# Six VectorE operations at other places of a hand-written order, and one PSUM tile in another bank

## The chip, the cores and the metric

The kernel runs on one core of a Trainium2 chip. The metric is the device time of one execution in microseconds. The engines are TensorE (PE, with its weight loads PEld), VectorE (DVE), ScalarE (ACT), GpSimd (POOL) and SyncE (SP). SP issues most DMAs and all transposing DMAs; POOL issues the DMAs that add to their destination.

## The reference, cut to what matters

The input is a sequence of 2048 positions with 640 channels. Two branches are computed from it and mixed by a sigmoid gate per position.

```python
def _A_ref(q, k, v, shift_k, ssm_k, ssm_D):      # long convolution
    k_shift = sum over 4 taps of shifted k times shift_k
    kv = k_shift * v
    y = irfft2(rfft2(kv padded) * rfft2(ssm_k padded))[:S]
    return q * (y + kv * ssm_D)

def _B_ref(x, w1, w2, w3, w4):                   # token-shift mixer and MLP
    h = gelu(layernorm(x) @ w1)
    x1 = x + concat(four quarters of h, shifted by 1, -1, 2, -2 positions) @ w2
    return x1 + gelu(layernorm(x1) @ w3) @ w4

g = sigmoid((x * gate_w).sum(-1))
out = g * a + (1 - g) * b                        # a, b: the two branches, x = A_q
```

## The kernel before

**The work.** Branch B runs over 16 tiles of 128 positions (names with t) or over 4 chunks of 512 positions (sc). `ln1` normalizes, `mm1` multiplies by w1, `mm2` by w2 and adds the residual (one VectorE operation per tile, a SCALAR_TENSOR_TENSOR at line 967 that reads PSUM), `ln2` normalizes again, `mm3` and `mm4` are the MLP, `base` stores a first part of the output. Branch A runs over 5 chunks of 128 channels (c). Its convolution is a folded discrete Fourier transform: `h_load` loads the filter, `h_fold` forms even and odd folds of it on VectorE and transposes them by a DMA, `h_even` and `h_chunk` finish its transform; `kv` does the same for the data (taps, product with v, fold, transposing DMA), `kv2` folds the transposed data once more (two operations, a sum and a difference), `x_fwd` transforms it on TensorE, `combine` prepares blocks. `unit(c)` multiplies the transforms block by block on VectorE: products go into two buffers TT[0] and TT[1] and are added to two accumulators, by VectorE (`tt`) or, where a bit of `ON` says so, by an accumulating DMA that POOL issues. `final` transforms back on TensorE, copies on ScalarE, folds on VectorE and stores.

**The order.** All operations are recorded one by one in the order of the source; an operation's number is its place in that record. Which operation depends on which is found from the memory they touch. `SEQUENCE` then lists all 1176 numbers in a hand-kept order. Each engine executes its own operations in the order in which they stand there, strictly one after the other; where an operation depends on one of another engine (or on an earlier one of its own, except on TensorE), `emit` puts a semaphore wait in front of it. A wait therefore holds everything behind it on that engine, and also, on SP, all DMAs behind it. `PLACES` gives each PSUM tile its first bank out of 8. A tile placed on a bank waits until the tile that was there before has been read:

```python
            if t is not None and t.place is None:
                t.place = places[t.idx]
                for b in range(t.place, t.place + t.n):
                    if tenant[b] is not None:
                        for u in tenant[b].users:
                            if ops[u].eng != "pe":
                                o.preds.setdefault(u, False)
                    tenant[b] = t
```

**The numbers that the text uses.**

| number | engine | what it is |
|---|---|---|
| 340 | DVE | `h_fold(1)`: main part of the second chunk's odd fold (128x1016) |
| 339, 341, 342 | DVE | small parts of the same fold; 343, a transposing DMA on SP, needs all of them and 340 |
| 290 to 293 | DVE | `h_even(0)` |
| 305, 306 | DVE | last two operations of `kv(0)`; 307 on SP transposes their result |
| 500, 504, 526, 508, 512, 530, 534 | DVE | `mm2`'s residual additions of tiles 0, 1, 4, 2, 3, 5, 6 |
| 230, 216 | PE | products whose PSUM tiles stand on the bank that 530 reads |
| 246, 256 | SP | transposes of the last chunk of `ln1`, behind 343 in SP's order |
| 390 | SP | load of the third chunk's filter, behind 256; 391 on DVE is the first to use it |
| 374, 375 | DVE | `kv2(1)`: the sum (374) and the difference (375) of the second chunk's even fold |
| 376 | PE | `x_fwd(1)`: first matmul that needs 374; 837 is the next `mm4` product |
| 637, 640 | POOL | accumulating DMAs of `unit(0)`, reading TT[0] |
| 639, 641 | DVE | `unit(0)`: product into TT[1] and its addition |
| 642, 643 | DVE | `unit(0)`: products into TT[0] and TT[1] |
| 644, 645 | DVE | additions of 642's and 643's products to the two accumulators |
| 646, 647, 648 | DVE, DVE, ACT | close the first half of `unit(0)`; 648 needs 647 |
| 649 to 654 | DVE | second half of `unit(0)`: 649, 650 first products; 651, 652 into TT[0], TT[1]; 653, 654 additions |
| 904, 905 | PE, ACT | `mm3(2)`: product into PSUM tile 149 and the gelu that reads it |
| 1021, 716 | PE | first matmuls into tiles 180 and 116, which follow on the banks concerned |

The product lines of the helper `tt` all appear at line 646, those of `act` at 656, the matmuls at 678, transposing DMAs at 234 and other DMAs at 237.

Of the kernel before, what the change touches and what calls it, by code (L numbers as in the profile page):

```python
# [433 lines left out]
def bass_gated_mix__ssm_conv_h3__mixer_s_mlp__prompt_kernel(  # L434
# [34 lines left out]
    def ps(n, cls):  # L469
# [4 lines left out]
                49, 14, 50, 131, 54, 15, 51, 36, 57, 55, 16, 66, 56, 17, 282, 65, 58, 18, 68, 336, 19, 69, 193, 20,  # L474
                67, 59, 71, 194, 41, 136, 21, 72, 42, 22, 70, 62, 60, 37, 133, 23, 61, 43, 35, 73, 135, 74, 295, 75,
                39, 63, 132, 83, 137, 64, 134, 81, 33, 76, 138, 78, 84, 139, 40, 91, 149, 82, 77, 87, 146, 97, 147,
                103, 150, 98, 79, 92, 88, 102, 80, 151, 95, 140, 107, 283, 148, 96, 105, 101, 108, 111, 152, 143,
                106, 119, 153, 44, 104, 286, 85, 120, 144, 112, 141, 123, 86, 145, 117, 154, 38, 99, 157, 155, 142,
                34, 113, 195, 158, 118, 196, 156, 166, 338, 114, 159, 168, 197, 198, 208, 109, 287, 337, 160, 100,
                288, 199, 169, 188, 167, 125, 284, 126, 110, 127, 128, 209, 180, 285, 289, 122, 93, 200, 206, 121,  # L480
                189, 201, 297, 190, 202, 191, 164, 94, 129, 207, 124, 182, 210, 298, 178, 181, 236, 165, 171, 192,
                89, 183, 172, 174, 161, 211, 299, 235, 179, 212, 162, 90, 175, 502, 203, 301, 503, 185, 186, 204,
                115, 170, 498, 205, 340, 213, 163, 499, 116, 300, 173, 214, 176, 291, 215, 524, 504, 525, 342, 500,
                505, 296, 302, 501, 506, 507, 177, 237, 184, 187, 510, 29, 526, 239, 30, 511, 508, 247, 349, 528,
                303, 240, 224, 249, 512, 220, 238, 304, 248, 532, 241, 225, 251, 306, 529, 221, 305, 533, 250, 242,
                290, 307, 243, 314, 513, 252, 317, 341, 530, 294, 318, 253, 293, 315, 292, 230, 319, 216, 339, 534,
                343, 316, 231, 245, 311, 312, 228, 232, 514, 217, 244, 233, 222, 255, 509, 246, 352, 234, 313, 218,
                515, 254, 516, 351, 223, 256, 308, 353, 219, 309, 331, 310, 332, 390, 320, 6, 328, 333, 321, 350,
                329, 322, 344, 323, 330, 271, 325, 226, 326, 272, 227, 273, 327, 274, 229, 265, 345, 324, 517, 355,
                261, 403, 519, 354, 259, 391, 393, 276, 266, 356, 522, 263, 275, 270, 518, 268, 277, 357, 257, 260,  # L490
                520, 521, 558, 278, 334, 279, 264, 559, 269, 358, 258, 554, 523, 348, 555, 267, 360, 262, 536, 359,
                406, 537, 560, 361, 371, 556, 372, 368, 346, 373, 369, 347, 395, 606, 576, 396, 281, 335, 370, 607,
                577, 538, 817, 365, 366, 392, 550, 367, 394, 551, 829, 608, 397, 562, 531, 552, 563, 527, 621, 635,
                535, 622, 539, 564, 602, 405, 540, 603, 632, 385, 386, 623, 823, 362, 387, 363, 541, 407, 542, 382,
                444, 383, 364, 604, 617, 409, 618, 633, 578, 816, 619, 824, 637, 384, 588, 543, 634, 579, 600, 408,
                445, 636, 592, 638, 548, 582, 399, 589, 640, 590, 398, 601, 547, 410, 584, 544, 549, 448, 596, 591,
                375, 585, 411, 594, 593, 597, 866, 598, 639, 595, 402, 422, 400, 641, 379, 583, 423, 380, 424, 586,
                446, 404, 401, 381, 642, 580, 643, 599, 587, 425, 644, 581, 426, 645, 416, 835, 651, 417, 419, 545,
                420, 646, 819, 818, 427, 449, 647, 546, 418, 374, 652, 820, 836, 648, 421, 457, 650, 376, 377, 872,
                837, 649, 378, 878, 458, 388, 561, 838, 654, 565, 653, 884, 447, 825, 412, 557, 553, 655, 839, 656,  # L500
                826, 821, 389, 657, 450, 566, 831, 661, 451, 460, 567, 414, 568, 413, 858, 827, 659, 415, 459, 832,
                663, 860, 830, 859, 658, 864, 867, 861, 665, 841, 462, 844, 879, 660, 667, 854, 865, 461, 845, 852,
                833, 569, 662, 463, 842, 453, 848, 664, 855, 856, 853, 464, 849, 666, 843, 862, 429, 857, 571, 465,
                850, 863, 669, 846, 851, 428, 574, 671, 452, 433, 847, 834, 434, 436, 466, 435, 439, 440, 455, 437,
                441, 430, 468, 431, 880, 467, 456, 668, 469, 570, 670, 881, 438, 454, 673, 572, 432, 672, 470, 625,
                443, 479, 882, 480, 674, 678, 473, 474, 914, 471, 676, 874, 481, 684, 873, 675, 472, 885, 475, 482,
                490, 491, 483, 493, 492, 677, 494, 886, 680, 495, 697, 679, 605, 442, 573, 887, 682, 609, 681, 575,
                487, 740, 888, 875, 683, 741, 484, 876, 485, 488, 738, 868, 489, 739, 486, 742, 869, 700, 689, 743,
                900, 610, 686, 699, 745, 894, 496, 908, 747, 624, 687, 611, 701, 870, 476, 906, 895, 685, 497, 901,
                890, 909, 744, 926, 620, 477, 927, 688, 892, 703, 690, 746, 691, 912, 626, 749, 627, 910, 891, 748,  # L510
                698, 478, 751, 612, 902, 907, 750, 920, 280, 752, 898, 911, 753, 903, 921, 896, 913, 757, 754, 758,
                904, 893, 755, 1008, 897, 915, 702, 988, 756, 989, 759, 999, 692, 760, 905, 1000, 628, 704, 840,
                899, 1021, 1001, 1022, 694, 990, 705, 716, 932, 717, 613, 1010, 629, 706, 933, 986, 1011, 630, 693,
                928, 980, 707, 718, 708, 766, 709, 696, 929, 1012, 762, 719, 761, 1023, 922, 1019, 767, 763, 614,
                1030, 764, 631, 930, 923, 962, 765, 768, 987, 720, 924, 769, 934, 615, 771, 616, 733, 695, 734, 723,
                773, 730, 735, 731, 889, 722, 935, 883, 732, 1013, 991, 931, 1002, 737, 916, 936, 1014, 721, 1003,
                770, 974, 917, 772, 918, 710, 711, 1024, 774, 712, 724, 919, 713, 1052, 714, 775, 725, 937, 1063,
                944, 715, 776, 822, 981, 727, 777, 1161, 728, 726, 1015, 950, 779, 1009, 778, 948, 784, 780, 992,
                945, 782, 960, 968, 956, 781, 961, 786, 729, 940, 1025, 1074, 783, 1016, 1086, 1064, 736, 938, 1098,
                949, 1041, 785, 957, 993, 946, 941, 1017, 963, 951, 792, 997, 1018, 939, 952, 1110, 994, 877, 1146,  # L520
                788, 947, 1004, 969, 871, 787, 942, 953, 975, 793, 1087, 1134, 789, 958, 1122, 790, 954, 959, 943,
                791, 1032, 794, 955, 828, 1020, 1033, 795, 1005, 982, 1034, 797, 998, 983, 995, 799, 1026, 964,
                1035, 1027, 801, 984, 1036, 1006, 803, 1031, 1028, 985, 965, 796, 1037, 798, 970, 966, 1038, 967,
                1099, 1039, 1053, 925, 800, 971, 1162, 1040, 1111, 802, 804, 976, 972, 805, 1147, 810, 996, 806,
                809, 973, 977, 808, 1112, 807, 978, 1100, 1101, 1042, 812, 979, 1113, 1102, 1043, 811, 1029, 1114,
                1044, 1103, 1075, 813, 1065, 1104, 1045, 814, 1066, 1135, 815, 1046, 1007, 1105, 1088, 1067, 1115,
                1047, 1089, 1116, 1106, 1068, 1048, 1076, 1107, 1049, 1077, 1069, 1090, 1108, 1136, 1050, 1078,
                1109, 1070, 1117, 1091, 1137, 1071, 1079, 1051, 1092, 1054, 1118, 1080, 1072, 1138, 1093, 1081,
                1119, 1055, 1094, 1139, 1073, 1082, 1120, 1163, 1140, 1056, 1121, 1083, 1141, 1164, 1095, 1142,
                1084, 1124, 1165, 1057, 1085, 1125, 1143, 1148, 1058, 1126, 1166, 1059, 1144, 1149, 1060, 1127,  # L530
                1145, 1096, 1150, 1128, 1097, 1061, 1129, 1130, 1151, 1170, 1123, 1062, 1155, 1167, 1156, 1168,
# [619 lines left out]
```

## Time and profile before

| | |
|---|---|
| median of 3 runs | 224.52 us (224.51 to 224.65) |
| profiled execution, its own time | 223.96 us |
| its span, first to last instruction | 222.1 us |
| busy: PE, DVE, ACT, POOL | 208.7, 211.7, 193.3, 54.2 us |
| mean granted TensorE clock | 0.995 |

The page of the profile gives shares of busy time, the chain of waits that ended last and the costliest groups. The timeline lists instructions in order of time, neighbours of one form merged, with the idle time before them and what ended it in square brackets; its first two columns are start and duration in us from the span's start. A stretch row gives, for a window of time, its length, the busy time and count of each engine, the granted clock, the share of the DMA engines and GB/s. A matmul's end is modelled in the records, so a full TensorE can still have small waits in it.

### The profile page before, as it was taken

The page shows a single profiled execution, that of the slowest core. Times are in us where ns is not written, and L with a number is a line of the kernel's source. Part 1 is how long each engine was busy: PE and PEld are TensorE (multiplying, and loading weights), DVE is VectorE, ACT ScalarE, POOL GpSimd, SP SyncE. Part 2 cuts the span into 40 slices and gives each one's busy share as a digit, 9 for nine tenths or more (in the row PEclk, how much of TensorE's full clock was granted, in tenths as well). Part 3 has the DMA queues.
Part 4 walks back from the last instruction along what each step waited for, and adds up shares of the span by engine and source line. Part 5 has one row for each costly group of instructions (what it writes and reads, how often), then busy time and mean ns, then how long its engine had stood idle before and what let it go on. Part 6 is the DMA issues. An engine that isn't in the chain of part 4 may idle for free.

```text
span 222.1 us, 3844 instructions
## 1 busy us (share of the span) xinstructions
PE 208.7 (94%) x1403; PEld 125.5 (57%) x1410; DVE 211.7 (95%) x417; ACT 193.3 (87%) x324; POOL 54.2 (24%) x57
## 2 busy tenths in 40 slices
PE   5899989989999999899999999999999999999970
PEld 2589755445665445565446575445667444677740
DVE  6999999989999986999999999999999999999993
ACT  2489999999899999799999999999977898566981
POOL 0512303200003100005130002164016427276431
PEclk9999999999999999999999999999999999999998
DMA  6999899999998999939958974599699979879896
GB/s 166 348 315 173 224 186 263 174 245 198 142 381 192 286 257 186 186 71 186 235 105 143 207 154 94 114 145 215 139 224 157 204 132 250 179 98 96 112 163 110
DMA packets 80561, 41.39 MB, mean 186 GB/s; under 512 B 59129, under 2 KB 77086, under 8 KB 80542
## 3 DMA queue, kind: packets, MB, share of 16 engines
q1 hardware_dynamic: 73872, 31.89, 64.2%
q0 software_dynamic: 6496, 9.18, 27.2%
q8 instruction: 11, 0.18, 0.3%
q10 hardware_dynamic: 174, 0.07, 0.1%
q14 instruction: 8, 0.07, 0.1%
HBM read 14.88 MB, written 5.77 MB: 93 GB/s over the span
## 4 chain that ended last, share of the span: by engine, by line
DVE 57%; PE 25%; DMA 8%; ACT 5%; issue 2%; SPq 1%
DVE arena L646 43%; PE PSall L678 25%; ACT arena L656 5%; DMA arena<-arena 5%; DVE arena L967 4%; DVE arena L651 4%; DVE arena L847 3%; DMA arena<-in_A_ssm_k_dram 2%; DVE arena L933 2%; DMA arena<-in_A_q_dram 2%; DVE arena L852 1%; SPq L237 1%; DVE arena L848 0%; SPq L234 0%; DVE arena L721 0%
## 5 line engine op out<-in xcount | busy, mean ns | idle before, releaser
L678 PE MATMUL PSall<-arena 128*128 128x512 bf16 (+5 forms) x1342 | 201.6, 309 | 5.4 <-DVE arena L646 3.0
L646 DVE TENSOR_TENSOR arena<-arena 128x1024 bf16<-128x1024 bf16 (+13 forms) x266 | 173.5, 715 | 4.3 <-DMA arena<-arena 2.9
L678 PEld LDWEIGHTS PSall<-arena 128*128 128x128 bf16 x1349 | 121.5, 98 | 85.0 <-DVE arena L646 4.2
L656 ACT ACTIVATE arena<-PSall 128x512 bf16<-128x512 f32 (+6 forms) x157 | 92.7, 661 | 10.8 <-PE PSall L678 4.9
L656 ACT ACTIVATE arena<-arena 128x640 bf16<-128x640 bf16 (+5 forms) x105 | 90.5, 888 | 3.9 <-DVE arena L646 3.6
L855 POOL TENSOR_TENSOR arena<-arena 128x2 f32<-128x2 f32 (+2 forms) x15 | 17.7, 1187 | 86.2 <-DVE arena L852 70.8
L237 POOL DMA_DIRECT2D out_dram<-arena x24 | 25.5, 1304 | 15.9 <-DVE arena L646 8.6
L656 ACT ACTIVATE arena<-PSall,arena 128x640 bf16<-128x640 f32 (+2 forms) x32 | 20.5, 658 | 8.6 <-PE PSall L678 8.6
L237 POOL DMA_DIRECT2D arena<-arena x14 | 12.4, 884 | 60.5 <-DVE arena L646 60.5
L651 DVE TENSOR_SCALAR arena<-arena 128x640 bf16<-128x640 bf16 (+6 forms) x37 | 13.2, 378 | 0.1
L967 DVE SCALAR_TENSOR_TENSOR arena<-PSall,arena 128x640 bf16<-128x640 f32 x16 | 12.8, 812 | 0.0
L847 DVE BATCH_NORM_STATS2 arena<-arena 128x6 f32<-128x320 bf16 x20 | 8.8, 479 | 1.0 <-DMA arena<-in_A_q_dram 1.0
L701 PE MATMUL PSall<-arena 128*128 128x512 bf16 x15 | 5.0, 484 | 2.2 <-DVE arena L698 2.2
L933 DVE TENSOR_SCALAR arena<-arena 32x256 bf16<-32x256 bf16 (+1 forms) x23 | 5.5, 237 | 0.3
L656 ACT ACTIVATION_READ_ACCUMULATOR arena<-arena 128x1 f32 x28 | 5.6, 201 | 0.0
L701 PEld LDWEIGHTS PSall<-arena 128*128 128x128 bf16 x15 | 1.6, 121 | 4.4 <-DVE arena L698 2.2
L908 PE MATMUL PSall<-arena 128*128 128x128 bf16 x40 | 3.4, 220 | 0.7 <-DVE arena L651 0.7
L908 PEld LDWEIGHTS PSall<-arena 128*128 128x128 bf16 x40 | 2.4, 97 | 1.4 <-DVE arena L651 1.4
L852 DVE SCALAR_TENSOR_TENSOR arena<-arena 128x2 f32<-128x2 f32 (+2 forms) x19 | 3.0, 159 | 0.0
L704 ACT ACT_TABLE_LOAD x1 | 1.3, 1283 | 1.3 <-PEq L1136 1.3
L848 DVE BATCH_NORM_AGGREGATE arena<-arena 128x2 f32<-128x12 f32 x10 | 1.9, 200 | 0.0
L967 DVE DVE_READ_ACCUMULATOR arena<-PSall,arena 128x1 f32 x16 | 1.2, 76 | 0.0
(19 smaller groups left out, 2.9 us busy)
## 6 DMA issues: line engine op xcount, KB each, us to landing
arena<-arena POOLq DMA_DIRECT2D x9, 512.0 KB, 6.4
arena<-in_A_ssm_k_dram SPq DMA_DIRECT2D x5, 512.0 KB, 4.3
arena<-in_A_q_dram SPq DMA_DIRECT2D x6, 320.0 KB, 5.5
arena<-in_B_w_dram SPq DMA_DIRECT2D x1, 1920.0 KB, 15.2
out_dram<-arena SPq DMA_DIRECT2D x16, 96.0 KB, 3.3
out_dram<-arena POOLq DMA_DIRECT2D x16, 96.0 KB, 4.8
arena<-in_A_q_dram SPq DMA_DIRECT2D x8, 192.0 KB, 3.5
out_dram<-arena POOLq DMA_DIRECT2D x8, 192.0 KB, 4.6
```

The source lines that it names most:

```text
L237: fn = lambda e: e.dma_start(out, in_, **kw)
L646: P.op(eng, lambda e: e.tensor_tensor(o, real(a), real(b), op), [a, b], [o], dve_ns(o, [a, b], 2) if eng == "dve" else 500)
L651: P.op(eng, lambda e: e.tensor_scalar(o, real(a), s1, s2, op0=op0, **({} if op1 is None else {"op1": op1})), [a] + aps, [o], dve_ns(o, [a] ...
L656: P.op("act", lambda e: e.activation(real(o), real(a), f, bias=bias, scale=scale, **({"accum_out": accum} if accum is not None else {})), ...
L678: fns.append(lambda e, l=l, r=r, i=i: e.matmul(real(o), l, r, start=(i == 0), stop=(i == last)))
L701: P.op("pe", lambda e: e.matmul(real(pw), warm[:, 0:128], warm[:, 128:640], start=True, stop=True), [warm], [pw], 427.0 if i < 14 else 216.0)
L847: P.op("dve", lambda e, o=o, i=i: e.bn_stats(o, i), [i], [o], 400)
L852: P.op("dve", lambda e: e.scalar_tensor_tensor(o, a, x, b, op0=op0, op1=op1), [a, b] + aps, [o], n_of(o) / 0.96 + 65)
L855: P.op("pool", lambda g: g.tensor_tensor(o, a, e, ALU.pow), [a, e], [o], dur)
L908: P.op("pe", [lambda e, c=c, pb=pb, xn=xn: e.transpose(real(pb)[:, 128 * c:128 * (c + 1)], xn[:, 128 * c:128 * (c + 1)], ident) for c in r ...
L933: P.op("dve", lambda e, o=hT[q, 4, c0:c0 + n], i=hx[q, :]: e.tensor_scalar(o, i, 1.0, None, op0=ALU.mult), [hx[q, :], *near], [hT[q, 4, c0 ...
L967: P.op("dve", lambda e: e.scalar_tensor_tensor(x, real(pr), 1.0, x, op0=ALU.mult, op1=ALU.add, accum_out=st[1, 0][:, t:t + 1]), [pr, x], [ ...
```

## The change

Two literals change, `SEQUENCE` and one entry of `PLACES`. `SEQUENCE` differs in many lines, since numbers of different engines are interleaved anew throughout. Taken engine by engine, the order of PE, ACT, POOL and SP is the same before and after. Only VectorE's order differs, in six numbers. Here is its order at the two places, before (-) and after (+):

```diff
  ... 185 186 204 170
- 340 213 173 214 291 504 342 500 302 184 187 526 508 303 512 304 241 251 306 305 242 290
+     213 173 214 291 504 342 500 302 184 187 526 508 303 512 304 241 251 306 305 242 290 340
- 252 341 530 293 292 339     534
+ 252 341     293 292 339 530 534
  245 228 514 ...
  ... 639 400 641 446 401
- 642 643 644 645 651 646 449 647 374 652     650 649 388 654 653
+ 643 374 645 642 644 646 449 647     652 651 650 649 388 654 653
  ...
```

So 340 moves behind 290, 530 behind 339, the three operations 643, 374 and 645 ahead of 642, and 651 behind 652. The moved tile:

```diff
-                7, 6, 2, 2, 4, 4, 0, 0, 4, 4, 2, 6, 0, 6, 3, 4, 1, 7, 2, 3, 5, 2, 2, 4, 4, 6, 5, 3, 6, 7, 3, 2, 1,
+                7, 6, 2, 2, 4, 4, 0, 0, 4, 4, 2, 6, 0, 6, 3, 4, 7, 7, 2, 3, 5, 2, 2, 4, 4, 6, 5, 3, 6, 7, 3, 2, 1,
```

This is tile 149, from bank 1 to bank 7. In bank 7 it follows tile 150. Tile 180 (banks 0 and 1) then follows tiles 145 and 80 instead of 145 and 149, and tile 116 (banks 6 and 7) follows 146 and 149 instead of 146 and 150. All other tiles keep bank and predecessor. No operation is added, removed or resized.

114 rows, old and new, of the table SEQUENCE are left out of this document.

## The prediction

> **What bounds the kernel now.** I read the page first (busy shares), then the chain of waits, then the busy time by stretch.
>
> ```profile
> PE 208.7 (94%) x1403; PEld 125.5 (57%) x1410; DVE 211.7 (95%) x417; ACT 193.3 (87%) x324; POOL 54.2 (24%) x57
> 45.32 4.03 DMA arena<-in_A_ssm_k_dram
> 75.04 10.82 DMA arena<-arena
> 85.89 13.21 DVE arena L646 x20
> 152.13 19.70 PE PSall L678 x132
> core 0: us, PE busy (x) PEld busy (x) DVE busy (x) ACT busy (x) POOL busy (x), PEclk, DMA share, GB/s
> 75.00:86.00 11.00, 10.95 (x52) 4.96 (x52) 8.14 (x12) 11.00 (x20) 0.88 (x1) 1.00 1.10 219
> 86.00:93.00 7.00, 5.93 (x40) 3.68 (x40) 7.00 (x12) 5.33 (x8) 0.00 (x0) 1.00 1.07 236
> 93.00:148.00 55.00, 54.83 (x316) 30.87 (x317) 54.93 (x80) 53.98 (x77) 11.95 (x9) 1.00 0.74 147
> 148.00:207.00 59.00, 58.87 (x372) 36.20 (x372) 58.46 (x85) 47.86 (x77) 24.60 (x28) 1.00 0.96 165
> ```
>
> VectorE (DVE) and TensorE (PE) are both nearly full. The stretches show where they are not. From 75 to 86 DVE is idle 11.00 - 8.14 = 2.86 us. From 86 to 93 PE is idle 7.00 - 5.93 = 1.07 and ScalarE (ACT) 1.67. From 93 to 207 DVE is idle 0.07 + 0.54 and PE 0.17 + 0.13 of 114 us. So after 93 us neither engine has room: what both gain before 93 stays gained up to the end, and what only one of them gains is mostly lost to the other. The granted clock is 1.00 in all four stretches. The chain agrees: it runs over a DMA into DVE at 85.89, and before that over the load that SP issues at 45.32, whose landing 45.32 + 4.03 = 49.35 DVE awaits. These two are the only places ahead of 93 us where I expect the change to act.
>
> **Part A: 643, 374 and 645 ahead of 642.** The rows at that place, from the timeline:
>
> ```profile
> 83.46 0.40 DVE L646 TENSOR_TENSOR arena<-arena 1x512 bf16<-1x512 bf16 x1
> 85.89 0.69 DVE L646 TENSOR_TENSOR arena<-arena 128x1024 bf16<-128x1024 bf16 x1 [2.02 <-DMA arena<-arena]
> 89.58 0.69 DVE L646 TENSOR_TENSOR arena<-arena 128x1024 bf16<-128x1024 bf16 x1
> 90.18 0.69 DVE L646 TENSOR_TENSOR arena<-arena 128x1024 bf16<-128x1024 bf16 x1
> 90.93 4.30 PE L678 MATMUL PSall<-arena 128*128 128x512 bf16 x28 [1.02 <-DVE arena L646]
> 90.30 0.63 ACT L656 ACTIVATE arena<-arena 1x512 bf16<-1x512 bf16 x1 [1.67 <-DVE arena L646]
> 41.55 0.16 DVE L852 SCALAR_TENSOR_TENSOR arena<-arena 128x4 f32<-128x4 f32 x1
> 41.62 1.10 DVE L651 TENSOR_SCALAR arena<-arena 128x640 bf16<-128x640 bf16 x2
> 42.76 1.83 DVE L646 TENSOR_TENSOR arena<-arena 128x2047 bf16<-128x2047 bf16 x2
> 75.04 0.88 POOL L237 DMA_DIRECT2D arena<-arena  x1 [3.43 <-DVE arena L646]
> ```
>
> The operation that starts at 85.89 is 642. It overwrites the buffer TT[0], which the accumulating DMA issued by POOL at 75.04 (640) still reads, and waits 2.02 us for its landing. 643 writes TT[1]; its last predecessor is 641, which ended before 83.46 + 0.40. 645 needs 643 and 641. 374 (at 90.18 above) needs a transpose whose result 375 already uses before 639 in DVE's order, and PE reads of the first chunk, long past. So all three can run inside the wait. An independent operation of this size costs 0.60 from start to start (89.58 to 90.18). Three take 1.80 and fit into 2.02; 0.2 us of the wait stays.
>
> Against it: without 643 and 645 between them, 642 to 644 and 644 to 646 become neighbours of which the second needs the first. An independent neighbour starts about 0.09 before the other ends (41.55 + 0.16 against 41.62), a dependent one 0.04 after it (41.62 + 1.10 against 42.76): 0.12 each, 0.24 in all. 651 goes behind 652; its successor 653 comes three operations later, so it costs nothing. Net on DVE: 1.80 - 0.24 = 1.56 us.
>
> Who else gains: PE's 376 waits for 374, 1.02 us at 90.93, and 374 now ends at about 85. That wait goes entirely; next in PE's order is 837, whose bank ACT frees before its own wait began at 90.30 - 1.67 = 88.63, so nothing is late behind it. ACT's 648 waits 1.67 for 647, which moves up by the 1.56. PE thus gains 1.02 here, and can regain the 0.17 and 0.13 of later idle time because DVE and ACT, on which it waits there, run 1.56 ahead. Bounds of part A: 1.02 (PE alone sets the rest) to 1.80 (no price for the new neighbours); I take DVE's 1.56, because DVE has the last long stretch to the end.
>
> **Part B: 340 and 530.**
>
> ```profile
> 24.99 0.68 DVE L646 TENSOR_TENSOR arena<-arena 128x1016 bf16<-128x1016 bf16 x1
> 28.96 7.63 PE L678 MATMUL PSall<-arena 128*128 128x320 bf16 x49 [0.77 <-DVE arena L967]
> 35.67 0.69 DVE L646 TENSOR_TENSOR arena<-arena 128x1024 bf16<-128x1024 bf16 x1
> 36.39 2.09 SPq L234 DMA_TRANSPOSE arena<-arena  x1
> 37.12 0.81 DVE L967 SCALAR_TENSOR_TENSOR arena<-PSall,arena 128x640 bf16<-128x640 f32 x1
> 38.20 0.49 DVE L646 TENSOR_TENSOR arena<-arena 1x512 bf16<-1x512 bf16 x2
> 38.72 3.52 SPq L234 DMA_TRANSPOSE arena<-arena  x1
> 38.07 0.72 PE L678 MATMUL PSall<-arena 128*128 128x512 bf16 x7
> 42.29 1.41 SPq L234 DMA_TRANSPOSE arena<-arena  x1
> 43.74 1.54 SPq L234 DMA_TRANSPOSE arena<-arena  x1
> 36.50:37.00 0.50, 0.50 (x5) 0.23 (x4) 0.50 (x2) 0.50 (x3) 0.49 (x1) 1.00 1.28 290
> 37.00:37.50 0.50, 0.50 (x4) 0.26 (x3) 0.50 (x4) 0.50 (x3) 0.50 (x1) 1.00 0.22 41
> 45.92 0.83 PE L678 MATMUL PSall<-arena 128*128 128x1 bf16 x12 [0.27 <-DMA arena<-arena]
> 47.34 1.50 PE L678 MATMUL PSall<-arena 128*128 128x1 bf16 x15 [0.59 <-DMA arena<-arena]
> 49.37 1.46 DVE L646 TENSOR_TENSOR arena<-arena 128x1 bf16<-128x1 bf16 x4 [0.45 <-DMA arena<-in_A_ssm_k_dram]
> ```
>
> 340 starts at 24.99 and takes its place from start to start, 0.61. Taken out there, everything up to 290 comes 0.61 earlier, 340 then fills that time, and from 252 on DVE is where it was. DVE's own sum is zero. Of what comes earlier, two things matter. 500 releases the bank for which PE waits 0.77 at 28.96; PE runs 0.6 ahead from there, which is lost again at 38 (below). And 305 (35.67, ends 36.36) releases SP's transpose 307 at 36.39: it can go at 35.78. In SP's queue behind it stands 343, held at 38.72 by 339, the second operation of the row at 38.20, which ends at 38.69. In the new order 339 no longer has 530 (0.74 from start to start) ahead of it and ends at about 37.94. Then come 246 and 256 (42.29, 43.74) and the filter load 390 (45.32), one directly behind the other. The DMA engines are full before and after, but at 37.0 to 37.5 their share is 0.22 against 1.28 just before: 307 came too late to follow without a gap. Issued 0.6 earlier it closes this gap, and the whole train moves up by about 0.5.
>
> What waits for the train: PE 0.27 at 45.92 and 0.59 at 47.34, DVE 0.45 at 49.37. So part B gives DVE 0.45. Bounds: 0 (the engines stay full, the train lands as before) to 0.61 (it moves by the whole advance of 307). I take 0.45, the whole wait of DVE, which lies nearest to the gap that closes.
>
> The price of 530: it ends at 38.68, not 37.94, and 230 and 216 of PE's order need its bank. PE started 230 at 38.07; now it can at about 38.74, up to 0.67 later, and ACT's reads behind it slip by as much at most. The cover is PE's wait for the train, 0.27 + 0.59 = 0.86, so the price is 0 as long as the train is no earlier than 0.19. If the train is 0.5 earlier, PE gains between 0.19 (all of 0.67 is felt) and 0.5 (ACT and other waits in between absorb it); with no cover at all the price would be 0.67 on PE. 531, which reads 530's result, stands far behind in ACT's order, next to reads of tiles that DVE finished later.
>
> After 49.4 us the 0.45 has to last to 85.89. DVE waits there for POOL's DMAs (issued when DVE is done, as the row at 75.04 shows) and once for ACT, all of which start from the same shifted work, so I carry it through.
>
> **The bank.** 149 goes from bank 1 to bank 7, so 1021, which starts at 152.13, no longer waits for ACT's 905.
>
> ```profile
> 151.51 0.57 ACT L656 ACTIVATE arena<-PSall 128x512 bf16<-128x512 f32 x1
> 77.19 4.51 SPq L234 DMA_TRANSPOSE arena<-arena  x1
> 81.75 4.80 SPq L234 DMA_TRANSPOSE arena<-in_A_v_dram  x1
> arena<-in_B_w_dram SPq DMA_DIRECT2D x1, 1920.0 KB, 15.2
> arena<-arena POOLq DMA_DIRECT2D x9, 512.0 KB, 6.4
> ```
>
> 905 ends at 152.08, so the old wait is real, but PE's idle time over the whole stretch from 148 to 207 is 0.13: the bank is worth 0 to 0.13. I take 0. Bank 7's last tile before it, 150, is read by ACT two operations ahead of the one that reads 152, and nobody else comes to wait.
>
> **Sum.** DVE: 1.56 + 0.45 + 0 = 2.01. PE: 1.02 + 0.19 to 0.5 + 0.3 = 1.5 to 1.8. The end needs both, since DVE's last operations wait for ACT's copies of PE's results (the chain ends with PE from 152.13); I take 1.9, between the two and nearer to DVE, whose rows are measured ends while PE's are modelled. The profiled execution, 223.96 with a span of 222.1, would come to 222.06 with 220.2. The median of the runs, 224.52, lies 0.56 above that execution; I subtract the same 1.9 and get 222.6.
>
> **Rivals.** A difference under 0.2% (0.45 us) is about what a measurement of this kernel cannot tell from none.
>
> *The train is not earlier (B lost).* For it: a DMA share of 1.28 says that the engines are full. Against: the gap at 37.0. Time 224.52 - 1.56 = 222.95.
>
> *The landing of 640 does not follow POOL's issue.* It took 75.04 to 85.86, where the median of such transfers is 6.4 us (the last row above); beside it ran the weight load of 1920 KB, landing 70.17 + 15.2 = 85.4, and SP's transposes from 77.19. If those decide, 642 keeps its time though DVE arrives earlier: again B is lost and A stays, 222.95. [...]
>
> *PE sets the end.* PE gains only its own 1.02 and DVE waits for it later: 223.5. For it: 54.83 of 55.00 busy. Against: its few later waits are for DVE and ACT.
>
> *The wait only moves.* 640 lands as much later as DVE is filled, or 643 has a wait that I overlooked: 224.1 to 224.9. Against: 641 and 375 are done.
>
> *Slower.* 640's landing falls behind the transpose of 81.75, whose issue alone takes 4.80. 642 would wait up to 4.8 us longer. It decides from 1.9 us, that is from a landing at 87.8. At the middle between 1.9 and 4.8, 3.35, the time is 224.52 - 1.9 + 3.35 = 226.0. For it: both transposes are queued before 640 lands. Against: DVE, POOL and SP all move the same way.
>
> **How the numbers follow.** Forecast 0.52 (222.2 to 222.9 by its own bounds); B lost, by either way, 0.17; PE sets the end 0.10; the wait only moves 0.08; slower 0.08; better than 222.2 0.05. Faster 0.52 + 0.17 + 0.10 + 0.05 = 0.84, same 0.08, slower 0.08. The range 221.9 to 223.6 holds the forecast, B lost, most of the PE case and half of the better one: about 0.8.
>
> **What would show it.** Part A: DVE's 2.02 us before 642 shrinks to about 0.2, PE's 1.02 and ACT's 1.67 at 90 vanish. Part B: SP's 36.39 and 38.72 become about 35.8 and 38.0, PE's idle time around 38.1 grows, DVE's 0.45 at 49.37 is gone. Wrong, if DVE's wait for that DMA is still over 1 us with the three operations ahead of it, or if idle time of PE after 93 grows by more than 0.5 us.

## The result, and the profile after

The changed kernel takes 222.01 us (median of 222.23, 221.55, 221.99 and 222.03) against 224.57 for the kernel before, run beside it: ratio 0.9883, 95% interval 0.9866 to 0.99. That is 2.56 us faster, or 2.2 to 3.0 by the interval. The forecast was 222.6, 1.9 us faster.

First the page of the changed kernel (busy time, the two costliest groups with the idle time ahead of them), then the same four stretches as before.

```profile
PE 209.6 (95%) x1410; PEld 125.9 (57%) x1410; DVE 211.6 (96%) x417; ACT 193.2 (88%) x324; POOL 55.9 (25%) x57
L678 PE MATMUL PSall<-arena 128*128 128x512 bf16 (+5 forms) x1349 | 201.3, 310 | 3.3 <-DVE arena L646 2.0
L646 DVE TENSOR_TENSOR arena<-arena 128x1024 bf16<-128x1024 bf16 (+12 forms) x266 | 173.4, 716 | 2.0 <-DMA arena<-arena 1.1
```

```profile
75.00:86.00 11.00, 11.00 (x53) 4.98 (x52) 9.88 (x15) 11.00 (x20) 0.88 (x1) 1.00 1.12 222
86.00:93.00 7.00, 7.00 (x50) 4.75 (x49) 6.93 (x11) 6.90 (x12) 0.00 (x0) 1.00 1.05 225
93.00:148.00 55.00, 55.00 (x316) 30.65 (x315) 54.93 (x82) 54.02 (x76) 11.97 (x9) 1.00 0.82 151
148.00:207.00 59.00, 59.00 (x382) 36.95 (x380) 58.47 (x87) 48.13 (x78) 25.49 (x27) 1.00 0.95 165
```

Busy times have hardly moved; idle time has gone. From 75 to 86 DVE is idle 1.12 us instead of 2.86. From 86 to 93 PE's 1.07 is gone, and of ACT's 1.67 there is 0.10 left. PE now has no idle time at all in these 132 us. The granted clock is 1.00 in all four stretches, as before.

The timeline of the changed kernel at the places that the prediction named (start, duration, work, and in brackets the idle time ahead; neighbours of one kind are merged, and idle times under 0.15 us are not printed, so a row without brackets has less than that ahead of it; the SP rows marked x2 join an issue with the next one, so 307 starts at 36.52, 343 at 38.91, 246 at 41.38, 256 at 43.58 and 390 at 45.16):

```profile
25.59 0.21 DVE L933 TENSOR_SCALAR arena<-arena 32x256 bf16<-32x256 bf16 x1
36.52 2.11 SPq L234 DMA_TRANSPOSE arena<-arena  x1
38.91 4.63 SPq L234 DMA_TRANSPOSE arena<-arena  x2
41.38 3.73 SPq L234 DMA_TRANSPOSE arena<-arena  x2
43.58 1.53 SPq L234 DMA_TRANSPOSE arena<-arena  x1
45.16 0.70 SPq L237 DMA_DIRECT2D arena<-in_A_ssm_k_dram  x1
39.47 10.71 PE L678 MATMUL PSall<-arena 128*128 128x1 bf16 x84 [0.88 <-DVE arena L967]
49.56 1.45 DVE L646 TENSOR_TENSOR arena<-arena 128x1 bf16<-128x1 bf16 x4
75.08 0.88 POOL L237 DMA_DIRECT2D arena<-arena  x1 [3.43 <-DVE arena L646]
80.56 11.63 DVE L646 TENSOR_TENSOR arena<-arena 128x2048 bf16<-128x2048 bf16 x17 [1.12 <-DMA arena<-arena]
85.76 6.56 PE L678 MATMUL PSall<-arena 128*128 128x512 bf16 x42
88.75 0.63 ACT L656 ACTIVATE arena<-arena 1x512 bf16<-1x512 bf16 x1
```

One thing has to be taken off before these times are compared. The first row is operation 170, a copy that stands at the same place in both orders. In the profile before it began at 24.86:

```profile
24.86 0.21 DVE L933 TENSOR_SCALAR arena<-arena 32x256 bf16<-32x256 bf16 x1
```

So this execution of the changed kernel was 0.73 us late on arrival, before any moved operation ran. Its VectorE had waited for one of the first loads, which it does not in the profile before:

```profile
6.05 0.49 DVE L847 BATCH_NORM_STATS2 arena<-arena 128x6 f32<-128x320 bf16 x1 [0.88 <-DMA arena<-in_A_q_dram]
```

Over all profiles of this study 170 starts between 24.81 and 25.59. I therefore read starts from 170 on. Then SP's 307 is 0.60 earlier (36.39 - 24.86 = 11.53 against 36.52 - 25.59 = 10.93), 343 0.54, 246 1.64, 256 and the filter load 390 0.89 each. DVE's wait for 390, which landed 0.75 earlier, is gone. Its wait of 2.02 before 642 is gone too: one unbroken row of 17 operations runs from 80.56 to 92.2. PE has no wait in its row from 85.76 to 92.3, where it waited 1.02, and ACT's 648 came from 90.30 to 88.75 with 0.10 left of its 1.67.

The end of the last instruction less the start of 170 fell from 222.08 - 24.86 = 197.22 to 220.35 - 25.59 = 194.76 us: 2.46, close to the 2.56 of the medians.

### The profile page after: what moved, and what is told of

It is laid out like the page before. It is cut to its first block, busy times and chain, and to the rows that moved or that the text cites. A ratio compares the mean times of both kernels' runs of the same rounds, so it can differ in the third digit from the quotient of the medians.

```text
span 220.3 us, 3850 instructions
## 1 busy us (share of the span) xinstructions
PE 209.6 (95%) x1410; PEld 125.9 (57%) x1410; DVE 211.6 (96%) x417; ACT 193.2 (88%) x324; POOL 55.9 (25%) x57
## 4 chain that ended last, share of the span: by engine, by line
DVE 73%; DMA 10%; PE 10%; ACT 3%; issue 2%; SPq 0%
DVE arena L646 63%; PE PSall L678 10%; DMA arena<-arena 8%; DVE arena L847 3%; DVE arena L651 3%; ACT arena L656 3%; DVE arena L967 2%; DMA arena<-in_A_q_dram 2%; DVE arena L933 1%; DVE arena L848 0%; DVE arena L852 0%; SPq L237 0%; DVE arena L721 0%
## 5 line engine op out<-in xcount | busy, mean ns | idle before, releaser
L678 PE MATMUL PSall<-arena 128*128 128x512 bf16 (+5 forms) x1349 | 201.3, 310 | 3.3 <-DVE arena L646 2.0
L646 DVE TENSOR_TENSOR arena<-arena 128x1024 bf16<-128x1024 bf16 (+12 forms) x266 | 173.4, 716 | 2.0 <-DMA arena<-arena 1.1
L678 PEld LDWEIGHTS PSall<-arena 128*128 128x128 bf16 x1349 | 121.7, 98 | 82.4 <-DVE arena L646 2.9
L656 ACT ACTIVATE arena<-PSall 128x512 bf16<-128x512 f32 (+6 forms) x157 | 93.1, 664 | 11.0 <-PE PSall L736 4.9
L656 ACT ACTIVATE arena<-arena 128x640 bf16<-128x640 bf16 (+5 forms) x105 | 90.4, 890 | 2.1 <-DVE arena L646 1.8
L855 POOL TENSOR_TENSOR arena<-arena 128x2 f32<-128x2 f32 (+2 forms) x15 | 19.5, 1306 | 84.1 <-DVE arena L852 67.9
L656 ACT ACTIVATE arena<-PSall,arena 128x640 bf16<-128x640 f32 (+2 forms) x32 | 20.5, 657 | 8.6 <-PE PSall L678 8.6
L967 DVE SCALAR_TENSOR_TENSOR arena<-PSall,arena 128x640 bf16<-128x640 f32 x16 | 12.7, 812 | 0.0
L701 PE MATMUL PSall<-arena 128*128 128x512 bf16 x15 | 6.4, 589 | 2.2 <-DVE arena L698 2.2
L656 ACT ACTIVATION_READ_ACCUMULATOR arena<-arena 128x1 f32 x28 | 5.7, 204 | 0.0
L967 DVE DVE_READ_ACCUMULATOR arena<-PSall,arena 128x1 f32 x16 | 1.2, 76 | 0.0
```

The lines of the kernel that those rows point to most:

```text
L646: P.op(eng, lambda e: e.tensor_tensor(o, real(a), real(b), op), [a, b], [o], dve_ns(o, [a, b], 2) if eng == "dve" else 500)
L656: P.op("act", lambda e: e.activation(real(o), real(a), f, bias=bias, scale=scale, **({"accum_out": accum} if accum is not None else {})), ...
L678: fns.append(lambda e, l=l, r=r, i=i: e.matmul(real(o), l, r, start=(i == 0), stop=(i == last)))
L701: P.op("pe", lambda e: e.matmul(real(pw), warm[:, 0:128], warm[:, 128:640], start=True, stop=True), [warm], [pw], 427.0 if i < 14 else 216.0)
L855: P.op("pool", lambda g: g.tensor_tensor(o, a, e, ALU.pow), [a, e], [o], dur)
L967: P.op("dve", lambda e: e.scalar_tensor_tensor(x, real(pr), 1.0, x, op0=ALU.mult, op1=ALU.add, accum_out=st[1, 0][:, t:t + 1]), [pr, x], [ ...
```

## Experiments

Each kernel is given as a difference in DVE's order. In their profiles the lines of the helpers stand four further on (L650 is L646 of the kernel before, L660 is L656, L682 is L678, L971 is L967). Runs scatter more than the effects of the small edits: the kernel before ran from 222.35 to 225.72 in these comparisons. So the table has a second measure beside the ratio, the end of the last instruction less the start of 170, one profile each; "by the profile" below means this column. The idle time of PE is that of the stretch from 50 to 207 us. In this column 0.31 is no wait: every profile but that of the changed kernel lacks seven of the 1410 matmul records (the pages count x1403 and x1410), and six of them leave holes of 0.05 us each in that stretch. So 0.31 there means the same as 0.00 in the changed kernel.

| kernel | median, us | ratio to before (95%) | 170 at | end less 170 | PE idle |
|---|---|---|---|---|---|
| before | 224.57 | 1 | 24.86 | 197.22 | 1.47 |
| changed | 222.01 | 0.9883 (0.9866 to 0.99) | 25.59 | 194.76 | 0.00 |
| a_only | 222.55 | 0.9917 (0.9885 to 0.9949) | 25.34 | 195.72 | 0.38 |
| b_only | 223.80 | 0.9976 (0.9952 to 0.9999) | 25.45 | 196.44 | 1.23 |
| bank_only | 224.20 | 0.9987 (0.9965 to 1.0008) | 25.38 | 197.52 | 1.37 |
| no_bank | 221.98 | 0.9895 (0.9866 to 0.9923) | 25.17 | 194.83 | 0.31 |
| only_374 | 223.75 | 0.9984 (0.9958 to 1.001) | 25.31 | 196.89 | 1.09 |
| only_643_645 | 223.34 | 0.9947 (0.9922 to 0.9971) | 25.26 | 195.75 | 0.44 |
| fill_637 | 222.24 | 0.9915 (0.9881 to 0.9949) | 25.44 | 194.92 | 0.31 |
| fill_637b | 222.17 | 0.9906 (0.9873 to 0.9939) | 25.27 | 195.14 | 0.37 |
| back_530 | 222.23 | 0.9914 (0.9883 to 0.9945) | 25.20 | 195.24 | 0.31 |
| back_340 | 222.78 | 0.9945 (0.9917 to 0.9972) | 24.81 | 195.95 | 0.46 |
| early_530 | 222.32 | 0.9915 (0.9891 to 0.994) | 25.10 | 195.15 | 0.31 |
| early_fill | 222.46 | 0.9926 (0.9903 to 0.995) | 25.14 | 195.30 | 0.37 |

**Part A alone.**

```diff
- 642 643 644 645 651 646 449 647 374 652     650
+ 643 374 645 642 644 646 449 647     652 651 650
```

> The kernel before with part A alone: 643, 374 and 645 ahead of 642, 651 behind 652; 340, 530 and the tile's bank as before. Theory 1 (the prediction's terms, B undersized): A is worth 1.56 us, 223.0, and DVE's 0.45 at 49.37 stays. Theory 2 (all of the gain is A, because PE loses both its 1.02 and what it waits for later): 222.0 to 222.3. Theory 3 (A is worth only what TensorE waited at 90.93): 223.5.

The timeline of this kernel, its waits of PE and DVE from 36 to 92 us, and ACT's 648:

```profile
47.65 2.58 PE L682 MATMUL PSall<-arena 128*128 128x1 bf16 x20 [0.61 <-DMA arena<-arena]
49.79 1.46 DVE L650 TENSOR_TENSOR arena<-arena 128x1 bf16<-128x1 bf16 x4 [0.38 <-DMA arena<-in_A_ssm_k_dram]
80.23 5.43 DVE L650 TENSOR_TENSOR arena<-arena 128x2048 bf16<-128x2048 bf16 x8 [0.52 <-DMA arena<-arena]
86.44 6.30 DVE L650 TENSOR_TENSOR arena<-arena 128x1024 bf16<-128x1024 bf16 x9 [0.78 <-DMA arena<-arena]
89.30 0.63 ACT L660 ACTIVATE arena<-arena 1x512 bf16<-1x512 bf16 x1 [0.38 <-DVE arena L650]
```

The waits at 47 and 49 stay, that of PE at 90 is gone and that of ACT has shrunk from 1.67 to 0.38, as Theory 1 has it. Of DVE's 2.02 before 642 there is 0.78 left where 0.2 was expected, because 637 landed 0.5 earlier in this execution (54.87 against 55.37 us from 170) and DVE came to 642's place earlier by that. The work itself has its predicted size: from 642 to 654 DVE takes 8.64 us before, 7.08 here and 7.06 in the changed kernel, 1.56 to 1.58 less. The gain is 1.50 us by the profile and 1.86 by the ratio (1.1 to 2.6), around the predicted 1.56. Theory 2's 222.0 to 222.3 is missed by little and the ratio does not exclude it; the profile's 1.50 speaks against it.

**Part B alone.**

```diff
- 170 340 213 ... 290     252 341 530 293 292 339     534
+ 170     213 ... 290 340 252 341     293 292 339 530 534
```

> The kernel before with part B alone: 340 behind 290, 530 behind 339; 642 to 652 in their old order, tile 149 in bank 1. Theory 1: 223.6 (B worth 0.9 to 1.0 here: 2.56 less 1.56), with TensorE dense from 39.5 on. By the prediction's own term 224.1. Theory 2: 224.5, since 642 still waits for the same landing of 640 at 85.86 and gives back whatever B brought; in that case DVE's wait ahead of 642 is over 2.3 us.

```profile
39.33 10.92 PE L682 MATMUL PSall<-arena 128*128 128x1 bf16 x84 [0.88 <-DVE arena L971]
85.53 6.72 DVE L650 TENSOR_TENSOR arena<-arena 128x1024 bf16<-128x1024 bf16 x11 [1.81 <-DMA arena<-arena]
90.58 2.67 PE L682 MATMUL PSall<-arena 128*128 128x512 bf16 x14 [0.78 <-DVE arena L650]
```

B brings 0.78 us by the profile and 0.54 by the ratio (0.0 to 1.1); from a_only to no_bank, which differ by B too, it brings 0.89 and 0.50. DVE has no wait for 390 any more. Theory 2 wanted a longer wait before 642; it is 1.81, not over 2.3. Counted from the start of 170, 642 stands at 85.53 - 25.45 = 60.08 where it stood at 85.89 - 24.86 = 61.03: the landing of 640 came forward too. One profile could show that by chance, since landings scatter (last section). But 640 was issued 49.5 us from 170 in the five kernels with part B unaltered, and landed at 58.8 to 60.3; in the seven that lack one or both of its halves it was issued at 50.0 to 50.4 and landed at 59.8 to 61.1. The means are 0.7 apart, in the issue and in the landing.

**The bank alone, and everything without the bank.** The one entry of `PLACES`, 1 to 7, in the kernel before; and 7 back to 1 in the changed kernel.

> The kernel before with tile 149 in bank 7 and nothing else changed. Theories 1 and 2: 224.5, within 0.13. Theory 3 (the bank carries the part of the gain that the two other terms don't explain): 223.9 to 224.0.

> The changed kernel with tile 149 back in bank 1. Theories 1 and 2: 222.0 to 222.1, as the changed kernel. Theory 3 (bank): 222.5 to 222.7; since TensorE has no idle time left after 39.5 us in the changed kernel, a wait of up to 0.5 us that was slack before could now count in full.

The bank alone is no different from before (the interval holds 1). Without it the change is what it was: 221.98 and 0.9895, inside the interval of the changed kernel, and 194.83 against 194.76 by the profile. Theory 3 fails in both directions.

**Part A in two halves.**

```diff
- 401     642 643 ... 647 374 652
+ 401 374 642 643 ... 647     652
```

> The kernel before with 374 alone ahead of 642 (643, 645, 651, 340, 530 and the bank as before). It fills 0.60 of DVE's 2.02 us before 642 and takes away the whole of TensorE's wait of 1.02 at 90.93. Theory D (DVE sets the end, as in the prediction): 0.60 us, 223.8. Theory P (TensorE sets the end): 1.02 us, 223.4.

```diff
- 401         642 643 644 645 651 646 449 647 374 652     650
+ 401 643 645 642     644         646 449 647 374 652 651 650
```

> The kernel before with 643 and 645 ahead of 642 and 651 behind 652; 374 stays behind 647. Fills 1.20 of the 2.02 us, less two new dependent neighbours of 0.12. Theory D: 0.96 us, 223.4; DVE's wait before 642 is 0.8. Theory P: TensorE's 376 waits for 374 0.96 us less, so 0.96 too; the two theories differ in the first of these two kernels, and here in whether the two gains add up to part A's (0.60 + 0.96 by D; by P they overlap, and the sum of the two is 0.4 us more than A's).

The waits of only_374 on DVE before 642, and on PE behind 93 us:

```profile
86.32 6.30 DVE L650 TENSOR_TENSOR arena<-arena 128x1024 bf16<-128x1024 bf16 x10 [1.30 <-DMA arena<-arena]
107.28 2.98 PE L682 MATMUL PSall<-arena 128*128 128x512 bf16 x13 [0.77 <-ACT arena L660]
```

374 alone takes away PE's 1.02 at 90.93, and PE gives 0.77 of it back at 107.28, waiting for ACT, which was not earlier by as much. What is left is 0.33 us by the profile and 0.36 by the ratio (-0.2 to 0.9): nearer to Theory D's 0.60 than to P's 1.02. Freeing PE alone brings little in the kernel before; there DVE and ACT hold it.

643 and 645 alone bring 1.19 by the ratio (0.65 to 1.75) and 1.47 by the profile, where 0.96 was expected. The profile shows why it is more than it should be: the expected wait of 0.8 before 642 is absent, in one row of 17 operations.

```profile
80.53 11.75 DVE L650 TENSOR_TENSOR arena<-arena 128x2048 bf16<-128x2048 bf16 x17 [0.70 <-DMA arena<-arena]
```

In this execution 640 landed 59.8 us after 170's start, by the trace, against 61.0 to 61.1 in the profiles of before, a_only, bank_only and only_374, although nothing ahead of its issue differs. So part of these 1.47 is luck of the landing. The two halves add up to 1.55 by the ratios (0.36 + 1.19), beside 1.86 for part A, and to 1.80 by the profiles, beside 1.50: whether they overlap by the 0.4 that Theory P asks for is not settled.

**DVE's last wait filled.**

```diff
- 411             639 400 641 446 401 643 374 645         642
+ 411 446 400 401 639     641         643 374 645 652     642    (fill_637)
+ 411 446 400 401 639     641         643 374 645 652 389 642    (fill_637b)
```

> The changed kernel with 446, 400 and 401 ahead of 639 (they fill DVE's wait of 1.1 us for the landing of 637) and 652 ahead of 642. 642 should start when 640 lands, as in the changed kernel, with 0.60 us of work more behind it done. Theory D: 0.6 us faster than the changed kernel, 221.4. Theory P (TensorE has no idle time after 39.5 us in the changed kernel): 222.0, no change, and DVE waits 0.6 more somewhere behind.

> The kernel of the run before (446, 400 and 401 ahead of 639, 652 ahead of 642) with 389 (0.86 us) ahead of 642 too, so that DVE never waits from 49 us on. Theory D: 1.1 us faster than the changed kernel, 220.9. Theory P: 222.0. A third way: 642 to 647 now come 0.6 to 0.7 us later, so ACT's 648 and what waits for it slip: 222.4 or more.

Who waited for whom from 20 to 207 us, on DVE in fill_637b, and the busy time from 50 to 207 us in fill_637b:

```profile
DVE arena L650 <- ACT arena L660: 0.3, 1, 0.3
50.00:207.00 157.00, 156.63 (x938) 91.87 (x942) 155.44 (x240) 144.17 (x215) 41.46 (x39) 1.00 0.91 177
```

The same row (busy time from 50 to 207 us) of the kernel before and of the changed kernel:

```profile
50.00:207.00 157.00, 155.53 (x923) 90.30 (x928) 153.24 (x234) 142.21 (x211) 39.52 (x39) 1.00 0.90 177
```

```profile
50.00:207.00 157.00, 157.00 (x944) 91.92 (x943) 155.07 (x239) 144.64 (x216) 41.48 (x39) 1.00 0.93 178
```

In fill_637b DVE waits for no DMA between 20 and 207 us, and 740 (first of `unit(2)`) comes 0.4 us earlier from 170 than in the changed kernel. The time does not follow: 222.17, ratio 0.9906 with an interval that holds the changed kernel's 0.9883. fill_637 kept 0.37 us of the wait for 637 and took 222.24. Both agree with Theory P: PE is busy for 156.6 to 157.0 of 157.0 us, of which 0.3 are the missing records, and DVE can't run further ahead than PE lets it. The third way is not excluded as a small part of it: in fill_637b ACT's 648 waits 0.71 us and stands 0.6 later from 170.

**The two halves of part B, undone one at a time in the changed kernel.**

```diff
- 290 340 252 341     293 292 339 530 534
+ 290 340 252 341 530 293 292 339     534    (back_530)
- 170     213 ... 290 340 252
+ 170 340 213 ... 290     252                (back_340)
```

> The changed kernel with 530 back behind 341 (340 stays behind 290). 339 then ends about 0.74 us later, and SP's 343 behind it; 530 ends about 0.8 earlier, so TensorE's stall ahead of 230 (1.25 us from 38.09) shrinks to about 0.5. Theory S (part B acts through SP's train of transposes): the wait of DVE for the load 390 comes back (0.4), TensorE waits again for the landings of 246 and 256, 222.5 to 222.9. Theory R (the stall of 230 costs as much as the train brings): 222.0 to 222.2.

> The changed kernel with 340 back behind 170 (530 stays behind 339). SP's 307 comes 0.61 later, 343 as in the changed kernel. Theory S: the gap of the DMA engines at 37 us is back and the train is later by up to 0.5; 222.5 to 222.8. If only 343 and what follows it count (the place of 339), 222.0 to 222.2, with no wait of DVE for 390.

DVE's wait for 390 in back_530 and then in back_340:

```profile
50.06 1.46 DVE L650 TENSOR_TENSOR arena<-arena 128x1 bf16<-128x1 bf16 x4 [0.80 <-DMA arena<-in_A_ssm_k_dram]
```

```profile
49.45 1.46 DVE L650 TENSOR_TENSOR arena<-arena 128x1 bf16<-128x1 bf16 x4 [0.57 <-DMA arena<-in_A_ssm_k_dram]
```

Either half undone brings the whole wait back, so the train needs both: 307 early by the move of 340, and 343 behind it early by the move of 530. back_530 loses little of the time (222.23; 0.48 us by the profile; by the ratios it can't be told from the changed kernel): the wait is that of Theory S, the time that of Theory R. PE's 230 stands 0.74 earlier there, which I take to be the reason. back_340 loses more (222.78; 1.19 by the profile), as Theory S has it: 230 is no earlier there, and the train is late.

**530 early as well, and both edits together** (the difference is that of early_530; early_fill has that of fill_637b besides).

```diff
- 290     340 252 341 293 292 339 530 534 245     228 514 ... 244
+ 290 530 340 252 341 293 292 339     534 245 244 228 514 ...
```

> The changed kernel with 530 directly behind 290 (ahead of 340) and 244 directly behind 245, ahead of 228 and 514. 530 ends about 0.9 us earlier than in the changed kernel, 339 about 0.74 later, 244, which releases SP's 246, 0.4 earlier. Theory P (from 39.5 us on TensorE sets the time): its stall of 1.25 us ahead of 230 falls to about 0.35; the landing of 246 (45.68 against a start of 46.46) limits what is kept to 0.78, that of 256 (47.15 against 47.33) to 0.18 unless the train is earlier by as much: 221.3 to 221.9. Theory D (DVE sets the time): 222.0 to 222.3.

> Both edits that aim at what is left: 530 and 244 early as in early_530, and DVE's wait for 637 filled as in fill_637b. If TensorE and DVE hold each other (each edit alone brings at most what the other engine lets through), the two together bring more than each alone: 221.0 to 221.5. If TensorE alone sets the end: as early_530.

PE's wait in early_530 between 36 and 50 us:

```profile
47.12 3.23 PE L682 MATMUL PSall<-arena 128*128 128x1 bf16 x23 [0.68 <-DMA arena<-arena]
```

PE starts 230 1.0 us earlier than in the changed kernel (from 170), and then waits 0.68 at 47.12 for the landing of 256. That landing is not earlier but 0.4 later (21.97 us from 170 against 21.56), because 530 now delays 339 again: 343 goes at 13.84 from 170, where it went at 13.32 in the changed kernel and at 13.87 before. The gain turned into a new wait: 222.32. Together with the filled wait it is 222.46. I expected 221.3 to 221.9 and 221.0 to 221.5; both expectations failed, and no version beat the changed kernel.

## Why the prediction was right, and what it sized wrong

The side was right, and so were the mechanism of part A, the path of part B up to DVE's wait for 390, and the order of the parts (A the most, B less, the bank nothing). How B's gain gets past the landing of 640 was argued from POOL's issue alone, and is still open. The gain came out 0.66 us larger than forecast.

*Part A*, predicted 1.56 (1.02 to 1.80): 1.50 by the profile and 1.86 by the ratio, and 1.56 to 1.58 by DVE's own time from 642 to 654. Of the three waits that it named, 2.02, 1.02 and 1.67, the changed kernel has 0.10 left, ACT's. This term stands.

*Part B* is the term that was too small, by the profiles: 0.45 predicted (0 to 0.61), 0.78 and 0.89 measured. By the ratios it is 0.5, and their intervals would let the excess lie in A as well; DVE's starts place it in B, 0.70 at 642 in the changed kernel. Its path up to DVE's wait for 390 went as written: SP's 307 0.60 earlier, the gap of the DMA engines closed, the load ahead of DVE's need. The gap shows when it is counted from 170: in the half microsecond from 12.5 to 13.0 us the share of the DMA engines is 0.42 to 0.50 in the six kernels with 340 at its old place and 1.09 to 1.17 in the eight others. Here that half microsecond in the kernel before, back_340, the changed kernel and b_only:

```profile
37.36:37.86 0.50, 0.50 (x5) 0.20 (x2) 0.50 (x1) 0.50 (x3) 0.50 (x2) 1.00 0.46 92
37.31:37.81 0.50, 0.50 (x4) 0.20 (x2) 0.50 (x3) 0.50 (x3) 0.50 (x2) 1.00 0.46 95
38.09:38.59 0.50, 0.50 (x3) 0.00 (x0) 0.50 (x3) 0.50 (x1) 0.50 (x2) 1.00 1.13 209
37.95:38.45 0.50, 0.49 (x3) 0.00 (x0) 0.50 (x3) 0.50 (x1) 0.50 (x2) 1.00 1.13 212
```

But the train moved by 0.9 at 256 and 390, not 0.5: 343, behind which 246 had to wait 3.57 us before (38.72 to 42.29), let it go after 2.47 (38.91 to 41.38). And I counted only the wait at 49.37. DVE had a second one, 0.20 at 67.12 for ACT, which shrank to 0.05, and 640 was issued and landed 0.7 earlier: that is how 0.5 us at 391 became 0.7 (changed kernel) to 0.95 (b_only) at 642, counted from 170.

*PE's sum* was too small too: 1.5 to 1.8 predicted, 2.5 measured. From 170, by the starts of the weight loads, its 230 is 0.65 later, 273 is 0.74 earlier, 376 1.99 and 1021 2.53. Its three rows, 0.27, 0.59 and 1.02, add up to 1.88. But from the start of the group ahead of each wait to the start of the next the trace shows 0.86, 1.06 and 2.76 us before, and 0.22, 0.32 and 1.47 after: 2.67 less. The rows count idle time from a modelled end of the matmuls ahead, and a group that is recorded as busy hides part of the stall. Less the 0.65 lost at 230, that is 2.0 of the 2.53. Most of the rest is PE's later waits for ACT, ahead of 852 (an `mm3` product) and 1021, 0.24 and 0.39 shorter by the same measure. The prediction counted 0.17 + 0.13 for them, of which 0.16 are holes of missing matmul records and only 0.14 were waits (0.07 each, at 107.10 and 152.13).

*The price of 530* was right in size: PE's 230 started 0.65 later from 170 (39.46 - 25.59 against 38.08 - 24.86), predicted up to 0.67. It was covered as written. early_530 agrees from the other side, though the train is later there too: with the stall gone, PE waits for the train instead.

*The bank* is worth 0 within the scatter, as taken. In bank_only PE is 0.23 earlier behind 1021, and 9 us later all but 0.08 of that is lost to another stall.

*The rivals.* "The train is not earlier" failed. "The landing of 640 does not follow POOL's issue" failed in its outcome, since 642 stood 0.95 earlier from 170 in b_only and 0.70 in the changed kernel. Its mechanism is not refuted: SP issued the weight load beside it 0.70 earlier as well (45.31 us from 170 before, 44.61 in both), so 640 could come forward by either, and no run here moves one without the other. "PE sets the end" was right for what it says of the changed kernel (the two fills), and wrong in its price of 223.5, since PE itself gained 2.5. In the kernel before it does not hold: only_374 gave PE's wait back behind ACT. The slower rival did not occur: 640 landed 10.8 us after its issue in both profiles (75.04 to 85.86, and 75.08 to 85.87 by the trace).

## What to carry to other kernels

Where two engines are both nearly full (here PE 94 and DVE 95% of the span), an edit counts if it frees both at the same place: 374 alone freed PE and brought 0.3, the three operations together freed PE, DVE and ACT and brought 1.5 to 1.9. Count what a transfer's earlier issue does to everything that is queued behind it (0.60 us at 307 came to 0.89 at 390), not only to the one wait that you can see, and measure a PE stall from start to start of its groups (by which 2.67 us went here) rather than by the idle time in its row (1.88). And stop when one engine has no idle time left: filling DVE's last 1.1 us (222.17), or freeing PE ahead of a landing that came no earlier (222.32), brought nothing against 222.01. Before you add up small idle times of PE, compare the number of matmul records in the two profiles (1403 and 1410 here).

## What was unexpected in the hardware

The landing of one and the same transfer scatters by over a microsecond. 640 landed 61.0 to 61.1 us from 170's start in four profiles in which B is not done, and 59.8 in a fifth (only_643_645); in fill_637b it was 58.8 where the changed kernel had 60.3. What decides it stays open, but it has a companion. In all fourteen profiles it landed within 0.25 us of a 96 KB store (824; 85.87 against 86.11 in the changed kernel), which SP issues directly behind the weight load of 1920 KB, about 4.5 us ahead of 640. In the kernel before:

```profile
70.17 0.37 SPq L237 DMA_DIRECT2D arena<-in_B_w_dram  x1
70.58 0.83 SPq L237 DMA_DIRECT2D out_dram<-arena  x1
out_dram<-arena SPq DMA_DIRECT2D x16, 96.0 KB, 3.3
```

The store landed at 85.89, 15.3 us after its issue, where the median of such stores is 3.3, and 640 at 85.86. So 640 looks tied to what SP queued ahead of it, though no run takes that away. The records of the kernel before show more of it: 640's last data packet ended at 83.1, and of the 16 updates of its semaphore six came at 83.1 to 83.4, but ten only at 85.7 to 85.9. In the changed kernel, though, the last data packet itself ended only at 85.5, so late updates are not the whole of it. The lesson for the reader is that an operation placed ahead of such a wait buys time in some executions and insurance in the others.
